# Redrawing the opening third of a written-out order, with one half pair's maximum subtracted on TensorE

## The chip, the cores and the metric

The kernel runs on one core of one Trainium2 chip. The metric is the device time of one execution in microseconds.

## The reference

Two layers follow each other. The first is attention in chunks: q, k and v are of shape (8 batches, 8 heads, 576 positions, 64), and each chunk of 64 positions attends to itself alone. The second takes the result as x of 576 x 512 per batch, multiplies x by a weight matrix, gates it with the sigmoid of a causal convolution of x over five positions, and multiplies by a second weight matrix.

```python
scores = scale * np.matmul(q_c, k_c.transpose(0, 1, 2, 4, 3))
scores = scores - np.max(scores, axis=-1, keepdims=True)
attn = np.exp(scores)
attn = attn / (np.sum(attn, axis=-1, keepdims=True) + 1e-09)
out = np.matmul(attn, v_c)
...
gate = 1.0 / (1.0 + np.exp(-gate_pre))
val = x @ w_val
return (gate * val @ w_out).astype(np.float32)
```

The two weight matrices and the convolution's taps are stored as 64-bit floating-point numbers; everything else has 32 bits.

## The kernel before, in words

The 8 x 576 positions are laid out as nine groups g of 512 positions (0 to 8). A group has two pairs p; a pair holds the heads of 256 of the 512 channels and has two halves b. The whole program is one list of pieces, ORDER, written out in the code: each piece is a short name with its indices, a small function issues its instructions, and every engine executes its own instructions in the order of this list (`run` keeps the program order). No engine overtakes itself, so an instruction that waits holds up everything behind it on its engine. SLOTS gives, in the order of the calls, the buffer that each tile takes; a transfer into a buffer waits until the buffer's last reader is done. All loads and stores are issued by SyncE, in the list's order. In the trace all pieces have one line, L139, that of `run`.

The pieces that matter here, with the engine in brackets:

- `lq`, `lk`, `lv g p [b]` load q, k, v of a pair or of its half (SyncE). `lw n c` loads one of the four row units c of the weights v (first matrix) or o (second), 512 KB each; `lc` loads the taps.
- `w1` to `w9`, `wa`, `wb`, `Q`, `wc` turn the 64-bit words of a unit into a high and a low 32-bit part: `w1` clamps the upper words (VectorE), `w2` scales them (ScalarE), `w3`, `w4`, `w7` work on their bits (VectorE), `w5` scales the lower words (ScalarE), `w8` multiplies them by the exponent (GpSimd, or VectorE as `w8D`), `w6` rounds the high part (ScalarE, or VectorE as `w6D`). The low part is a sum, either on GpSimd or VectorE (`wa`, `wb`) or on TensorE (`Q`, three matmuls that the trace shows as four) and a copy out of PSUM (`wc`).
- `S g p b` computes the scores of a half pair: sixteen small products, 32 records in the trace (TensorE, into PSUM).
- `mx` takes the maximum of each row (VectorE). Then there are two ways: `sb` subtracts it (VectorE), `ex` exponentiates (ScalarE) and `sm` sums and inverts (VectorE); or `ng` scales the maximum by -1/8 (VectorE) and `ea` does exponential, subtraction and sum by ScalarE alone, one exponential and one read-out for each of the 16 (or, of a half, 8) blocks. `ra` and `rr`, or `rc`, then add the small constant and invert.
- `nm` multiplies by the inverse sum (GpSimd; VectorE as `nmD`), `T` transposes (TensorE), `ec` copies the result out of PSUM (ScalarE), `A` multiplies by v (TensorE), `xr`, `xd` and `xc` make x in a high part, a low part and whole (ScalarE, VectorE, ScalarE).
- `V g m c [term]` is one (or, without a term, three) of the matmuls of 128 x 512 of the first weight product: high by high (0), low weight by high x (1), high weight by low x (2). For the first group all terms are listed one by one, in an order of their own. `P` is the same for the second product.
- `k0` and `k` are the taps of the convolution (ScalarE and VectorE), `sg` the sigmoid, `vc`, `gs`, `gr`, `gd` the gating, `oc` and `st` the way out.
- `W n s` keeps TensorE at work with n matmuls of 512 and s of 64 columns on zeros; nothing reads the result.

The opening, which the change redraws, is the first 290 pieces of the list, up to `vc 1 0`; from `V 1 2 3` on the order stays. The first half pairs treated are those of (0, 1), since the weights' units v 3 and v 2 belong to pair 1.

## Time and profile before

| | us |
|---|---|
| median of 3 runs | 280.78 |
| lowest and highest | 280.31, 281.07 |
| span of the profiled execution | 279.6 |
| TensorE, busy in it | 268.9 |
| VectorE, busy in it | 239.5 |
| ScalarE, busy in it | 198.7 |
| GpSimd, busy in it | 59.4 |

The profile is one execution's; its time is given as its span alone, which stands 1.18 us below the median of the runs. In the profile PE is TensorE's matmuls, PEld its weight loads, DVE VectorE, ACT ScalarE, POOL GpSimd and SP SyncE. Tiles are named without their numbers: z and ys are the general buffers, b the PSUM banks, mx and rs the row statistics, e_row the exponentials. A bracket behind an instruction tells how long its engine stood idle before it, and what ended that; "issue" is idle time for which the profile shows no wait. A busy TensorE is not one at its peak, since the ends of matmuls overlap.

### The profile page before, as it was taken

The numbers are of one execution on the slowest core, as the hardware profiler recorded it, in microseconds if no ns is written. First come the engines' busy times: TensorE is split into PE (matmuls) and PEld (weight loads), VectorE is DVE, ScalarE is ACT, GpSimd is POOL, SyncE is SP. The second block draws the span as 40 slices with busy tenths as digits, with TensorE's granted clock in tenths as the row PEclk, the third lists the DMA queues.
The fourth block names the chain that finished last, engine by engine and source line by source line (L and its number), as shares of the span: only waits on it lengthen the run. The fifth ranks groups of instructions, "written<-read, shape, count | busy, mean of one in ns | idle before, by whom it ended". The sixth has DMA issues, their size and how long they took to land.

```text
span 279.6 us, 7851 instructions
## 1 busy us (share of the span) xinstructions
PE 268.9 (96%) x3370; PEld 216.6 (77%) x3370; DVE 239.5 (86%) x303; ACT 198.7 (71%) x368; POOL 59.4 (21%) x58
## 2 busy tenths in 40 slices
...
GB/s 224 395 409 406 406 407 409 290 225 108 281 149 37 192 150 338 189 131 30 2 292 88 2 5 2 0 0 2 0 0 0 4 0 0 16 212 0 241 209 225
DMA packets 14754, 42.46 MB, mean 152 GB/s; under 512 B 1536, under 2 KB 1792, under 8 KB 14720
## 3 DMA queue, kind: packets, MB, share of 16 engines
...
q8 instruction: 26, 0.43, 0.6%
...
## 4 chain that ended last, share of the span: by engine, by line
PE 89%; DMA 8%; issue 1%; SPq 0%; ACT 0%
PE b L139 89%; DMA z<-in_v 4%; DMA z<-in_moe_w_val 2%; DMA z<-in_q 2%; SPq L139 0%; ACT z L139 0%
## 5 line engine op out<-in xcount | busy, mean ns | idle before, releaser
L139 PE MATMUL b<-z,v_hi 128*128 128x512 f32 x288 | 97.3, 403 | 1.3 <-issue 1.1
L139 PE MATMUL b<-o_hi,z 128*128 128x512 f32 (+1 forms) x296 | 94.5, 391 | 0.0
L139 DVE SCALAR_TENSOR_TENSOR ys<-ys,cw 128x511 f32<-128x511 f32 (+7 forms) x104 | 84.5, 863 | 0.1
L139 ACT COPY z<-b 128x1024 f32<-128x1024 f32 (+2 forms) x53 | 50.3, 970 | 38.3 <-PE b L139 35.5
L139 PEld LDWEIGHTS b<-z,v_hi 128*128 128x128 f32 x288 | 53.8, 188 | 14.5 <-issue 1.7
L139 PEld LDWEIGHTS b<-o_hi,z 128*128 128x128 f32 x296 | 55.1, 188 | 12.6
L139 PE MATMUL b<-o_lo,z 128*128 128x512 f32 (+1 forms) x148 | 57.4, 388 | 0.0
L139 PE MATMUL b<-z,v_lo 128*128 128x512 f32 x144 | 55.9, 394 | 0.0
L139 POOL TENSOR_TENSOR z<-e_row,rs 128x1024 f32<-128x1024 f32 (+1 forms) x15 | 27.0, 1804 | 47.2 <-DVE rs L139 17.0
L139 PEld LDWEIGHTS b<-o_lo,z 128*128 128x128 f32 x148 | 27.8, 188 | 5.9
L139 PEld LDWEIGHTS b<-z,v_lo 128*128 128x128 f32 x144 | 27.1, 188 | 5.4
L139 POOL TENSOR_TENSOR z<-ys,z 128x1024 fp32r<-128x1024 f32 x4 | 10.0, 2527 | 96.9 <-ACT z L139 96.9
L139 ACT ACTIVATE ys<-ys 128x1024 f32<-128x1024 f32 x16 | 16.8, 1059 | 11.0 <-DVE ys L139 10.8
L139 ACT ACTIVATE e_row<-b,mx 128x64 f32<-128x64 f32 x80 | 23.7, 345 | 0.4 <-DVE mx L139 0.4
L139 DVE TENSOR_TENSOR z<-b,z 128x1024 fp32r<-128x1024 f32 (+1 forms) x19 | 22.0, 1161 | 2.3 <-ACT z L139 1.3
L139 ACT CAST z<-ys 128x1024 fp32r<-128x1024 f32 x16 | 16.5, 1048 | 9.0 <-DVE ys L139 9.0
L139 DVE TENSOR_REDUCE mx<-b 128x16 f32<-128x1024 f32 (+1 forms) x19 | 21.6, 1144 | 1.3 <-PE b L139 1.1
L139 PEld LDWEIGHTS b<-z,z 64*64 64x64 f32 x960 | 15.7, 135 | 7.8 <-DMA z<-in_k 2.6
L139 PE MATMUL b<-z,z 64*64 64x64 f32 x960 | 17.6, 221 | 3.7 <-DMA z<-in_q 3.0
L139 ACT CAST z<-b 128x1024 fp32r<-128x1024 f32 (+1 forms) x19 | 18.7, 991 | 2.1 <-PE b L139 2.1
L139 ACT ACTIVATE ys<-ys,cw 128x512 f32<-128x512 f32 (+1 forms) x25 | 19.2, 811 | 0.0
L139 ACT ACTIVATION_READ_ACCUMULATOR e_row<-b,mx 128x1 f32 x80 | 19.0, 238 | 0.0
...
## 6 DMA issues: line engine op xcount, KB each, us to landing
...
```

The lines of the kernel that those rows point to most:

```text
L139: return tc.keep_in_program_order(fn(*args, **kwargs))
```

## The change

The list's first 290 pieces are replaced by 285 others, and the buffers in SLOTS are given out anew. The matmuls of the first weight product, the scores, transposes and products with v stay the same in number. Several pieces take another form:

- The first half pair (0, 1, 0) no longer uses `ng`, `ea`, `ra`, `rr`. `mh` splits its maximum into a high and a low part (two small VectorE instructions), `M` subtracts both from the scores in PSUM (four matmuls of 256 columns with minus the identity), `exM` exponentiates the whole half at once, and `sm` sums on VectorE. The second half (0, 1, 1) uses `rc` for `ra` and `rr`, and `nmD` for `nm`.
- For v 1, v 2, v 0 and o 3 a new piece `w58` does `w5` and `w8` in one VectorE instruction. `w1` of v 0 and of all four o units goes to GpSimd (`w1G`). `w2` of v 1 and o 0 goes to VectorE, `w6` of v 3 and v 0 to ScalarE.
- The loads come in another order: q and k of (0, 1, 0) ahead of v 2, the unit v 0 behind v of (0, 1), q and k of (1, 1) and the unit o 3 behind v of (0, 0).
- The three warm matmuls `W 3` move from behind `S 0 1 0` to the start of the list, directly ahead of `W 9 22`.

The functions get an index for half a unit; no piece of the list uses it. The core of the diff, the list up to where it stays and the functions that compute something new:

```diff
-ORDER = """zw,lw v 1,zr 1,zr 0,lc,zi,zs 0,zs 1,lw v 3,lw v 2,w1 v 1,w5 c 0,w1 c 0,w2 v 1,w3 v 1,w5 v 1,w4 v 1,w2 c 0,w3 c 0,w5 v 3,
-w7 v 1,w1 v 3,w6 v 1,w8D v 1,w2 v 3,w4 c 0,w3 v 3,W 9 22,Q v 1,lk 0 1 0,lq 0 1 0,w1 v 2,w4 v 3,w2 v 2,w3 v 2,w5 v 2,w6D v 3,
-S 0 1 0,lk 0 0 0,lk 0 1 1,lq 0 1 1,lq 0 0 0,lk 0 0 1,lq 0 0 1,w4 v 2,wc v 1,mx 0 1 0,w6 v 2,w7 c 0,ng 0 1 0,w7 v 2,ea 0 1 0,ra 0 1 0,
-W 3,S 0 1 1,w8D v 2,S 0 0 0,mx 0 1 1,w8D c 0,w9,ng 0 1 1,w7 v 3,S 0 0 1,lw v 0,lk 1 0,lq 1 0,lv 0 1,lw o 3,ea 0 1 1,ra 0 1 1,
-rr 0 1 0,Q v 2,w8 v 3,mx 0 0,nm 0 1 0,sb 0 0,Q v 3,w5 v 0,w1 v 0,ex 0 0,T 0 1 0,w3 v 0,rr 0 1 1,S 1 0 0,wc v 2,sm 0 0,
-nm 0 1 1,S 1 0 1,ec 0 1 0,w2 v 0,A 0 1 0,lk 1 1,lq 1 1,lv 0 0,lv 1 0,wc v 3,mx 1 0,T 0 1 1,nm 0 0,xr 0 1 0,ec 0 1 1,
-V 0 2 2 0,sb 1 0,V 0 3 2 1,w5 o 3,A 0 1 1,xc 0 1 0,xr 0 1 1,w4 v 0,T 0 0,xc 0 1 1,xd 0 1 0,V 0 2 3 0,w6D v 0,V 0 3 3 0,
-ec 0 0,V 0 2 3 1,w1 o 3,S 1 1 0,w7 v 0,ex 1 0,xd 0 1 1,A 0 0,w8 v 0,k0 0 2,sm 1 0,S 1 1 1,wa v 0,xc 0 0,V 0 0 2 0,V 0 2 2 1,
-V 0 0 3 1,V 0 0 2 1,xr 0 0,mx 1 1,V 0 1 2 0,nm 1 0,V 0 0 3 2,V 0 3 3 1,k0 0 0,V 0 3 2 2,V 0 2 3 2,xd 0 0,V 0 3 1 0,
-V 0 1 2 1,V 0 0 0 0,V 0 3 3 2,V 0 3 0 0,lw o 0,lw o 2,lw o 1,w5 o 0,k0 0 3,ng 1 1,k 0 0 1,T 1 0,k0 0 1,wbD v 0,V 0 0 0 2,
-w2 o 3,V 0 3 2 0,k 0 0 2,V 0 2 1 1,ec 1 0,V 0 2 0 0,V 0 0 1 0,k 0 3 1,V 0 1 0 0,V 0 2 0 1,ea 1 1,V 0 2 0 2,w3 o 3,V 0 2 1 2,
-k 0 1 1,V 0 3 1 1,V 0 0 2 2,V 0 1 1 1,w4 o 3,V 0 3 0 1,V 0 2 2 2,V 0 3 1 2,w1 o 1,A 1 0,k 0 0 3,w7 o 3,w1 o 0,V 0 1 3 2,
-V 0 1 1 2,lk 2 0,k 0 3 2,V 0 0 3 0,V 0 0 0 1,lq 2 0,lq 2 1,V 0 0 1 1,k 0 2 1,V 0 3 0 2,V 0 2 1 0,xr 1 0,rc 1 1,S 2 0 0,
-w1 o 2,S 2 0 1,nm 1 1,vc 0 1,xd 1 0,V 0 1 0 2,V 0 1 3 0,lv 3 1,lv 1 1,lq 8 1,lv 2 1,lk 2 1,lk 4 0,lq 6 1,lq 3 0,lv 2 0,
-lk 3 0,lq 3 1,w6 o 3,V 0 0 1 2,lq 4 0,V 0 1 3 1,mx 2 0,xc 1 0,V 0 1 0 1,V 0 1 1 0,V 0 1 2 2,w8 o 3,T 1 1,lk 3 1,vc 0 0,
-sb 2 0,V 1 2 0,ec 1 1,V 1 0 0,w3 o 1,k 0 2 2,ex 2 0,A 1 1,k 0 1 2,w2 o 2,sm 2 0,S 2 1 0,xr 1 1,S 2 1 1,V 1 1 0,w5 o 2,
-xd 1 1,nm 2 0,w2 o 0,V 1 1 1,w2 o 1,V 1 0 1,mx 2 1,xc 1 1,V 1 3 2,ng 2 1,k 0 3 3,V 1 0 3,ea 2 1,w3 o 2,V 1 0 2,k 0 0 4,
-V 1 1 2,k 0 1 3,T 2 0,w4 o 1,V 1 2 2,w7 o 1,k 0 2 3,V 1 3 3,k 0 1 4,V 1 3 0,k 0 2 4,ec 2 0,V 1 3 1,w4 o 2,V 1 1 3,w3 o 0,
-k 0 3 4,S 3 0 0,sg 0 0,S 3 0 1,rc 2 1,w7 o 2,A 2 0,nm 2 1,mx 3 0,vc 1 0,V 1 2 3,xr 2 0,sb 3 0,V 1 2 1,w8 o 2,sg 0 1,T 2 1,
...
+ORDER = """zw,zr 1,zr 0,W 3,lw v 1,w1 v 1,lc,lw v 3,w1 c 0,w2 c 0,w3 c 0,w3 v 1,w2D v 1,w4 v 1,w7 v 1,w6 v 1,w1 v 3,w2 v 3,W 9 22,w3 v 3,
+w58 v 1,w4 v 3,w7 v 3,lq 0 1 0,lk 0 1 0,S 0 1 0,mx 0 1 0,lw v 2,w1 v 2,zi,zs 1,mh 0 1 0,zs 0,Q v 1,w2 v 2,w4 c 0,lk 0 1 1,
+w3 v 2,lq 0 1 1,S 0 1 1,w4 v 2,w7 v 2,M 0 1 0,wc v 1,exM 0 1 0,w6 v 2,w5 v 3,w8 v 3,lq 0 0 1,mx 0 1 1,w58 v 2,lk 0 0 1,S 0 0 1,
+ng 0 1 1,lk 0 0 0,lq 0 0 0,S 0 0 0,sm 0 1 0,nm 0 1 0,w6 v 3,mx 0 0,Q v 2,Q v 3,ea 0 1 1,T 0 1 0,sb 0 0,lq 1 0,ex 0 0,rc 0 1 1,
+w7 c 0,wc v 2,nmD 0 1 1,lk 1 0,sm 0 0,S 1 0 1,T 0 1 1,ec 0 1 0,S 1 0 0,mx 1 0,lv 0 1,A 0 1 0,ec 0 1 1,A 0 1 1,wc v 3,xr 0 1 0,
+lw v 0,xd 0 1 0,w1G v 0,xr 0 1 1,xd 0 1 1,w2 v 0,sb 1 0,w3 v 0,w4 v 0,xc 0 1 0,nm 0 0,T 0 0,V 0 1 3 2,V 0 1 2 0,xc 0 1 1,
+V 0 1 3 1,w5 c 0,ec 0 0,lv 0 0,V 0 0 3 2,V 0 1 2 1,V 0 3 2 0,A 0 0,ex 1 0,lw o 3,lq 1 1,lk 1 1,S 1 1 0,lk 2 1,S 1 1 1,V 0 2 2 2,
+V 0 2 2 1,w6 v 0,xr 0 0,V 0 0 1 0,V 0 3 0 1,V 0 3 1 0,w1G o 3,xc 0 0,V 0 2 3 1,w8D c 0,V 0 2 0 1,V 0 2 2 0,w7 v 0,w9,V 0 3 2 2,
+w58 v 0,sm 1 0,V 0 3 3 1,xd 0 0,V 0 0 3 1,V 0 1 3 0,V 0 2 0 2,V 0 3 1 1,wa v 0,nm 1 0,T 1 0,mx 1 1,V 0 0 0 0,w2 o 3,V 0 3 0 2,
+wbD v 0,w3 o 3,ng 1 1,V 0 1 2 2,k0 0 1,k 0 1 4,k0 0 3,k 0 3 1,V 0 1 1 2,lw o 2,V 0 2 1 1,V 0 0 1 2,w4 o 3,k 0 1 1,k0 0 0,
+V 0 3 3 2,V 0 1 0 1,V 0 2 1 2,k0 0 2,k 0 0 2,k 0 2 4,V 0 0 2 0,k 0 0 1,w3 o 2,ec 1 0,V 0 3 3 0,V 0 0 2 1,V 0 0 3 0,V 0 1 0 2,
+k 0 1 3,V 0 3 1 2,V 0 0 2 2,ea 1 1,rc 1 1,V 0 0 1 1,V 0 0 0 2,V 0 1 0 0,w1G o 2,V 0 1 1 0,V 0 0 0 1,nm 1 1,V 0 1 1 1,vc 0 0,
+lk 2 0,lq 2 0,S 2 0 0,S 2 0 1,w6 o 3,lv 1 0,A 1 0,mx 2 0,xr 1 0,lw o 0,V 0 2 3 0,V 0 2 0 0,V 0 2 3 2,V 0 3 2 1,lw o 1,w1G o 1,
+w2 o 2,sb 2 0,xd 1 0,V 0 2 1 0,lq 2 1,V 0 3 0 0,vc 0 1,lq 3 1,T 1 1,ec 1 1,w4 o 2,w7 o 3,S 2 1 1,V 1 3 0,k 0 3 3,k 0 0 4,lv 1 1,
+ex 2 0,sm 2 0,A 1 1,S 2 1 0,xc 1 0,V 1 3 1,xr 1 1,V 1 0 0,xd 1 1,w5 o 2,lq 4 0,mx 2 1,lk 3 1,w5 o 0,w2 o 1,ng 2 1,w58 o 3,
+k 0 3 2,xc 1 1,w3 o 1,k 0 1 2,k 0 2 2,V 1 1 1,V 1 3 3,k 0 3 4,lv 2 0,w3 o 0,w4 o 1,V 1 1 2,V 1 0 3,lq 6 1,V 1 2 0,w1G o 0,
+w2D o 0,w7 o 1,V 1 0 1,k 0 0 3,V 1 1 0,ea 2 1,lk 4 0,V 1 0 2,w7 o 2,k 0 2 1,lv 2 1,nm 2 0,T 2 0,V 1 1 3,rc 2 1,lq 3 0,lk 3 0,
+S 3 0 1,lv 3 1,k 0 2 3,S 3 0 0,mx 3 0,ec 2 0,A 2 0,V 1 3 2,nm 2 1,V 1 2 2,vc 1 0,lq 8 1,sg 0 0,V 1 2 3,xr 2 0,sb 3 0,V 1 2 1,
...
     def mh(g, p, b=None):
         m = cols(mxs[g, p, b], b)
-        r = pool.tile([P, 2, 16], F32R, name=f"mr{small['mx'] % 6}")
+        small["mr"] = small.get("mr", 0) + 1
+        r = pool.tile([P, 2, 16], F32R, name=f"mr{small['mr']}")
...
-                            rhs=kk[r, b, c], start=True, stop=True, skip_group_check=True)
+                            rhs=kk[r, b, c], start=each or (first and u == a == 0), stop=True, skip_group_check=True)
...
+    def w1(n, c, b=None, on=V):
+        words(n, c)
+        run(on.tensor_scalar, out=part(wt[n, c], b), in0=part(raw[n, c][1], b).bitcast(F32), scalar1=WIDEST, scalar2=-WIDEST,
             op0=ALU.min, op1=ALU.max)
...
+    def w58(n, c, b=None):
+        run(V.scalar_tensor_tensor, out=rest(n, c, b)[1], in0=part(raw[n, c][0], b), scalar=2.0**-52,
+            in1=part(wt[n, c], b), op0=ALU.mult, op1=ALU.mult)
```

## Rows read from the trace of the kernel before

**Rows 1.** the page, busy us of the engines (share of the span), instructions.
```profile
PE 268.9 (96%) x3370; PEld 216.6 (77%) x3370; DVE 239.5 (86%) x303; ACT 198.7 (71%) x368; POOL 59.4 (21%) x58
```

**Rows 2.** the chain that ended last: start us, us, what.
```profile
13.77 11.88 DMA z<-in_v
...
31.90 52.88 PE b L139 x1014
84.78 0.90 issue
```

**Rows 3.** windows: length, busy us (instructions) by engine, granted clock, DMA share, GB/s.
```profile
5.00:10.00 5.00, 2.35 (x27) 1.03 (x27) 4.23 (x12) 3.91 (x8) 0.00 (x0) 1.00 0.95 344
...
25.00:30.00 5.00, 4.57 (x133) 3.91 (x123) 4.15 (x5) 4.62 (x8) 4.46 (x3) 1.00 1.03 410
```

**Rows 4.** timeline of SyncE's transfers: start us, us, queue, tensor, issues merged.
```profile
13.77 1.67 SPq L139 DMA_DIRECT2D z<-in_v  x2
16.32 3.39 SPq L139 DMA_DIRECT2D z<-in_moe_w_out  x3
20.66 0.33 SPq L139 DMA_DIRECT2D z<-in_k  x1
...
25.66 1.61 SPq L139 DMA_DIRECT2D ys<-in_v  x2
```

**Rows 5.** timeline of TensorE (PE, and PEld its weight loads), 0 to 32 us.
```profile
1.19 4.16 PE L139 MATMUL b<-warm 128*128 128x512 bf16 x31 [1.19 <-DVE warm L139]
...
2.02 0.15 PEld L139 LDWEIGHTS <-warm 128*128 128x128 bf16 x1 [0.28 <-issue]
...
9.82 0.69 PE L139 MATMUL b<-z,z 64*64 64x64 f32 x32 [1.39 <-DMA z<-in_q]
...
14.51 1.12 PE L139 MATMUL b<-z,ident 128*128 128x512 f32 x2
...
17.26 0.63 PE L139 MATMUL b<-ident,z 128*128 128x128 f32 x4
...
22.90 1.06 PE L139 MATMUL b<-ident,z 128*128 128x128 f32 x8 [0.32 <-DVE e_row L139]
...
25.78 1.63 PE L139 MATMUL b<-z,z 64*64 64x64 f32 x96 [0.43 <-DMA z<-in_v]
27.34 0.50 PE L139 MATMUL b<-z,v_hi 128*128 128x512 f32 x1
27.68 0.86 PE L139 MATMUL b<-z,v_lo 128*128 128x512 f32 x3
28.38 0.62 PE L139 MATMUL b<-z,v_hi 128*128 128x512 f32 x2
...
31.90 0.73 PE L139 MATMUL b<-z,v_hi 128*128 128x512 f32 x2 [0.17 <-issue]
```

**Rows 6.** groups of VectorE (DVE) by shape, names and shapes xcount | busy us, mean ns.
```profile
L139 DVE TENSOR_SCALAR z<-z 128x512 uint32<-128x512 uint32 x16 | 6.7, 417 | 0.0
L139 DVE SCALAR_TENSOR_TENSOR z<-z 128x512 uint32<-128x512 uint32 x8 | 5.5, 685 | 0.3 <-ACT z L139 0.3
```

**Rows 7.** timeline, ea 0 1 1, ex 0 0, sm 0 0, nm 0 0.
```profile
14.40 0.29 ACT L139 ACTIVATE e_row<-b,mx 128x64 f32<-128x64 f32 x1
...
17.68 1.04 ACT L139 ACTIVATE e_row<-e_row 128x1024 f32<-128x1024 f32 x1
...
18.82 1.24 DVE L139 TENSOR_REDUCE rs<-e_row 128x16 f32<-128x1040 f32 x1 [0.92 <-ACT e_row L139]
...
20.58 1.90 POOL L139 TENSOR_TENSOR z<-e_row,rs 128x1024 f32<-128x1024 f32 x1 [1.55 <-PE b L139]
```

**Rows 8.** group of GpSimd (POOL) by shape: busy us, mean ns.
```profile
L139 POOL TENSOR_TENSOR z<-z,z 128x512 f32<-128x512 f32 x5 | 7.4, 1479 | 6.0 <-DVE z L139 6.0
```

**Rows 9.** timeline of ScalarE, first of the sixteen ea 1 1 and what follows them.
```profile
32.67 0.32 ACT L139 ACTIVATE e_row<-b,mx 128x64 f32<-128x64 f32 x1
...
37.31 1.12 ACT L139 CAST z<-b 128x1024 fp32r<-128x1024 f32 x1
```

232 lines of the change are left out of this document (129 added, 103 removed), and 12 rows, old and new, of the table z.

## The prediction

> **What bounds the kernel now.** I read the page first. TensorE is busy for 96% of the span [rows 1], which only says that there is little to win unless its work shrinks, so the question is where its 10.7 us of idle time lie. The chain of waits answers it [rows 2]: from 31.90 us TensorE works without a break for 52.88 us, stands 0.90 us at 84.78, and works on to the end. Before 25.65 us the chain runs through transfers (the row of 11.88 us is the last of them). The kernel has thus two parts: an opening of some 26 us in which weights, q and k come in and are prepared, and a TensorE-bound rest whose matmuls the change doesn't touch. A change of the opening is worth what it brings forward the moment from which TensorE has work without a gap; everything behind shifts with it.
>
> In the opening the windows show a second full resource: from 5 to 10 us the DMA engines are at a share of 0.95, from 25 to 30 us still at 1.03 with 410 GB/s [rows 3]. The list of SyncE's transfers shows how they follow each other [rows 4]: counted from the start, issue 28 comes at 25.66 us, just as TensorE stops waiting for the v tile of (0, 0) [rows 5], which is issue 20 (13.77 us). Each issue waits for the landing of the one eight before it, so landings can be read off later issues: the 16th lands at 19.39 (the last of the three issues that the row at 16.32 merges and that ends at 19.71), the 17th at 20.66, the 20th at 25.64.
>
> **The change part by part.**
> *The transfers.* The new order issues as many transfers, in another order, and by the code none of the first twenty waits for a buffer. The 13th to 20th are full 512 KB tiles before and after; so I let the nth land when the nth landed. q and k of the first half pair move ahead of the weights v 2: S 0 1 0, at 9.82 before after a wait of 1.39 us [rows 5], should start near 8.4 (the 3rd and 4th transfers' place). lw v 0 goes from 13th to 16th: 19.4. lv 0 0, on which TensorE waited, goes from 20th to 17th: 20.7, long before its use. The 20th is now lk 1 1, which S 1 1 0 needs.
>
> *The first half pair.* Out go one ng, eight ACT pairs of exponential and read-out, ra and rr; in come two small VectorE copies (mh), four matmuls of 256 columns (M), one exponential of 512 elements (exM), and a VectorE sum (sm). The trace has no M. Four matmuls at half the pitch of a 512-column one (three in 0.70 us before 28.38, [rows 5]) are 0.5 us; were each as slow as one of the eight of Q v 2 and Q v 3 (2.75 us from 14.51 to 17.26), 1.4 us; less than nothing is excluded, as they are added. I take 0.5: they are the shortest of that engine's kind. They stand where TensorE waits for data anyway, so neither end is on the path.
>
> *The weights.* w5 and w8 of four units become one VectorE instruction (w58), w1 of five units goes to POOL, w2 of two to VectorE, w6 of two from VectorE to ACT, nm of the second half from POOL to VectorE. With 0.42 us for a scalar operation and 0.69 for a two-operand one [rows 6]: w58 of v 0 and o 3, which VectorE did not do before, +1.4; nm +0.7; sum of the half pair +0.9; two w2 +0.8; five w1 -2.1; two w6 -0.8; VectorE gets about 1 us more by the end of the redrawn part. ACT gets less: the eight pairs alone were 2.3 us (sixteen take 4.64 us, [rows 9]), and four w5 go as well. VectorE stands idle 0.85 us from 25 to 30 us and 0.77 us from 5 to 10 us [rows 3]; the extra 1 us is covered by such holes, with little to spare, and would be on the path without them.
>
> *The half pairs up to T 0 0.* ea 0 1 1 can't begin before its maximum, for which VectorE is as late as before: 14.4, ending near 16.8, as it did. ex 0 0 came at 17.68, behind w5 v 0 and ra; now it only waits for sb 0 0, about 17.1. Its sum sm 0 0 moves from 18.82 to about 18.2 and is done, with its reciprocal, at 19.7 instead of 20.3 [rows 7]. nm 0 0 runs on POOL, but now behind w1G v 0, which can't start before v 0 has landed at 19.4. A scalar operation on 512 elements is not in POOL's list: 0.42 us below (what VectorE needs for one, [rows 6]), 1.48 us above (POOL with two operands, [rows 8]); I take 0.7, half the upper row, since it reads one operand instead of two. nm 0 0 then runs from 20.1 to 22.0 (1.90 us, [rows 7]), and T 0 0 starts at 22.1 instead of 22.90 [rows 5]. Six V matmuls, the ACT copy ec 0 0 and A 0 0 follow; about 3.1 us later TensorE is at S 1 1 0: 25.2. There it waits for lk 1 1 until 25.64. So w1G may take up to 1.1 us before it costs anything. ACT has a wait for it too: w2 v 0 needs w1G v 0, and both xc of (0, 1), ec 0 0 and with them the first V queue behind it; ACT comes to it only near 21.0, behind ec, wc and both xr, so this wait is hidden as long as w1G takes less than 1.6 us.
>
> *The gain.* I compare the start of the tenth V matmul, since both orders have then done the same work on TensorE. Before: A 0 0 and a block of S still follow the wait at 25.78, and the tenth V starts at 28.38 [rows 5]. After: S 1 1 0 and S 1 1 1 from 25.67, 0.52 us each (96 small records, three blocks, fill 25.78 to 27.34), then the 7th V at 26.71, the tenth 0.81 us on at 27.52. Gain 0.86 us. Behind it, the old order loses 0.17 us at the end of T 1 0 (idle before 31.90); since no data is named as its cause, I count it on neither side. ACT's sixteen ea pairs of (1, 1) take 4.6 us (32.67 to 37.31, [rows 9]); in the new order they start behind ec 1 0 near 32.1 and end near 36.7, A 1 0 needs their bank near 37.1, T 1 1 needs nm 1 1 behind them near 39.1 and is reached near 39.6: close but in time. Further on, A 1 1 waits for ec 1 1 and V 1 3 3 for xd 1 1; by the same counting each may be late by 0.2 to 0.3 us, against as much that the order saves by putting S 2 0 beside A 1 0 (one change of shape on TensorE less). I set these off.
>
> The sum against the profiled execution: 279.6 - 0.86 = 278.7 us of span. The median of the runs is 280.78, 1.2 us above this span, and the same 1.2 us stand around it after: 279.9.
>
> **The clock.** TensorE's first warm matmuls of 512 columns are 0.43 us apart (weight loads of 0.15 us with 0.28 us between, as at 2.02), which is 1.2 GHz; the V matmuls at 0.23 us run at 2.4 GHz, and the window from 5 to 10 us grants 1.00, over the idle 1.39 us before 9.82 too [rows 3, 5]. The three warm matmuls that stood in the middle of the opening (W 3) are now at its start, where the block that ended at 5.35 (1.19 + 4.16) ends 0.7 us later, and the idle stretch up to S 0 1 0 is some 2.3 us. The rows show no fall after 1.39 us; for 2.3 us there is none, so I take no fall and keep the other end for the range. By the Trainium skill (TensorE: Matmul & The Clock Gate, "What's actually happening") the throttled state is the default and activity is what lifts it, so a longer idle stretch speaks against this change; the trace before neither shows nor excludes it. By that rule the third rival below would be the outcome.
>
> **The rivals.**
> *No change (280.6).* The new order leaves POOL, ACT and VectorE almost no slack from T 1 0 to A 1 1, and my counting lets each operation start as soon as it can. For it: the counted waits at A 1 1 and V 1 3 3, the extra 1 us on VectorE, w1G at its upper 1.48 us (T 0 0 0.8 us later, S 1 1 0 0.35 us). Against: ACT loses over 2 us of work, and the window from 25 to 30 us shows idle VectorE. Together 0.7 us: 280.6.
> *The gap at 84.78 goes as well (279.0).* 0.90 us without a named releaser; were it a matter of how instructions fall in TensorE's stream, eight more of them could remove it: 279.9 - 0.9. It could as well stay, which I think likelier.
> *The clock falls (281.8).* Place: the idle stretch before S 0 1 0. It decides if TensorE is still at the lower level when Q v 2 and Q v 3 come, near 14.3. These took 2.75 us (14.51 to 17.26, [rows 5]) and would take 5.5; T 0 1 0, both A 0 1, xr and T 0 0 move by about 2.7 us, of which 0.5 us is hidden by the wait for lk 1 1: S 1 1 0 would come at 27.9 instead of 25.67, and the gain of 0.86 us would turn into a loss of 1.4 us, with everything behind at full clock. If the clock is back after the first of the two Q, half of the 2.75 us falls away and the loss is near zero. I take 1.0: 281.8.
>
> **How the numbers follow.** A measurement of this kernel can tell about 0.3% (0.84 us) from no change. Forecast 279.9: 0.50, spread from 279.3 to 280.4, so slightly more than half of it counts as faster. No change 280.6: 0.24, mostly within 0.3%. Gap gone, 279.0: 0.13, faster. Clock, 281.8: 0.13. Faster: 0.28 of the forecast, 0.02 of the second case, 0.13 of the third: 0.43. Slower: 0.09 of the clock and 0.08 of the second case, if more waits add up than I counted: 0.17. Within 0.3%: the rest, 0.22 + 0.14 + 0.04 = 0.40. The range, 278.9 to 281.4, takes in the third case's value and the forecast's and second case's spread, and of the clock's case the mild half; what it leaves out is that case's other half and a few in a hundred at either end.
>
> **What would show it.** Right: SyncE's 28th issue again near 25.6; T 0 0 near 22.1; TensorE waiting for in_k just before 25.7 and the tenth V near 27.5; granted clock 1.00 and Q v 2 at 1.4 us; from there no TensorE idle above 0.3 us up to the first V of the old order (V 1 2 3, which should come some 0.9 us earlier). Wrong: POOL's w1G over 1.1 us with T 0 0 later than 22.5; matmuls of 512 columns 0.43 us apart near 14 us; waits of TensorE for ACT or VectorE from 30 to 46 us that sum to the gain; VectorE without any idle time through that stretch.

## The result and the profile after

The changed kernel takes **282.69 us** (median of 7 executions, 281.76 to 285.38) against 281.07 (280.31 to 281.70) of the kernel before beside it: a ratio of 1.0076, interval 1.0051 to 1.0100, so 0.8% slower where 0.3% faster was forecast. Three of the 7 had a mean clock of 0.988 to 0.994 and took 283.5 or more; ratios here leave out executions that were over 1.5% above the fastest, so where many were, a median lies above what its ratio says.

The profiled execution (282.69 us, span 280.9, clock 1.0) shows no single culprit. In the changed kernel the line of `run` is L137. TensorE's opening in the timeline, which answers to [rows 5]:

```profile
9.29 0.69 PE L137 MATMUL b<-z,z 64*64 64x64 f32 x32 [3.01 <-DMA z<-in_k]
...
12.54 0.71 PE L137 MATMUL b<-mr,signed 128*128 128x256 f32 x4
...
14.63 0.69 PE L137 MATMUL b<-z,z 64*64 64x64 f32 x32 [0.67 <-DMA z<-in_q]
...
23.02 1.09 PE L137 MATMUL b<-ident,z 128*128 128x128 f32 x8 [1.29 <-POOL z L137]
...
28.27 0.40 PE L137 MATMUL b<-z,v_lo 128*128 128x512 f32 x1
...
30.84 0.27 PE L137 MATMUL b<-ident,z 128*128 128x128 f32 x1
31.39 0.92 PE L137 MATMUL b<-ident,z 128*128 128x128 f32 x7 [0.28 <-issue]
...
44.49 0.93 PE L137 MATMUL b<-z,z 64*64 64x64 f32 x49 [0.17 <-issue]
...
60.40 1.09 PE L137 MATMUL b<-ident,z 128*128 128x128 f32 x8 [1.03 <-POOL z L137]
```

S 0 1 0 (first line) starts at 9.29 instead of the forecast 8.4, T 0 0 at 23.02 instead of 22.1, and the tenth V matmul at 28.27 instead of 27.52. S 0 0 0, the second half of pair (0, 0), starts at 14.63; in the kernel before that pair's second half came at 13.88:

```profile
13.88 0.69 PE L139 MATMUL b<-z,z 64*64 64x64 f32 x32 [0.69 <-DMA z<-in_q]
```

S 1 1 0 waits for no transfer; the forecast had it wait for lk 1 1. What follows is new: two waits "issue", for nothing the profile shows, inside T 1 0 (31.39) and inside A 1 1 (44.49, after 47 of its 64 matmuls), and 1.03 us ahead of T 2 1.

Three points split the loss, because both orders have done the same work at each (the tenth V; V 1 2 3, up to which from the tenth V on both have 53 V pieces, 3 T, 6 S and 3 A; the last matmul):

| | before | after | change | forecast |
|---|---|---|---|---|
| tenth V | 28.38 | 28.27 | -0.11 | -0.86 |
| V 1 2 3, later by | 28.71 | 29.55 | +0.84 | 0 |
| end of the last matmul, later by | 219.58 | 220.12 | +0.54 | 0 |

The chain that ended last answers to [rows 2]:

```profile
56.98 1.07 ACT z L137
...
58.19 2.17 POOL z L137
60.36 0.04 issue
60.40 217.55 PE b L137 x2420
```

From 60.40 us TensorE works to the end without a break: the 0.90 us at 84.78 [rows 2] are gone. So the last row of the table is +1.1 at T 2 1 (2.59 us from V 1 2 3 to it, 1.49 before), -0.9 for that gap, and +0.3 spread thinly.

Three more profiles of the changed kernel were taken in the experiments. In all four the tenth V starts at 27.75 to 28.27 us, so 0.1 to 0.6 of the 0.86 us were gained against the one profile of the kernel before; from there to V 1 2 3 it takes 29.39 to 29.71 us instead of 28.71, and to T 2 1 again 2.59. The first profile, the one shown here, has the latest opening of the four.

SyncE's timeline answers to [rows 4]:

```profile
8.49 1.00 SPq L137 DMA_DIRECT2D z<-in_q  x2
...
11.86 0.33 SPq L137 DMA_DIRECT2D z<-in_moe_w_val  x1
...
20.27 0.33 SPq L137 DMA_DIRECT2D z<-in_q  x1
...
25.37 1.61 SPq L137 DMA_DIRECT2D z<-in_q  x2
```

The first row is the 12th and 13th issue, which wait for the landings of the 4th and 5th (8.48 and 9.15 us). The second is the 16th, the unit v 0 (value-weight chunk 0 from here on); the third, the 24th, waits for its landing: 20.25 instead of 19.39. The 28th issue comes at 25.37, as forecast (25.6). VectorE's and GpSimd's timelines answer to [rows 7, 8]:

```profile
18.99 1.24 DVE L137 TENSOR_REDUCE rs<-e_row 128x16 f32<-128x1040 f32 x1
20.26 0.25 DVE L137 RECIPROCAL rs<-rs 128x16 f32<-128x16 f32 x1
```

```profile
20.43 0.67 POOL L137 TENSOR_SCALAR z<-z 128x512 f32<-128x512 f32 x1 [3.12 <-DMA z<-in_moe_w_val]
21.07 1.90 POOL L137 TENSOR_TENSOR z<-e_row,rs 128x1024 f32<-128x1024 f32 x1
...
49.38 1.08 POOL L137 TENSOR_SCALAR z<-z 128x512 f32<-128x512 f32 x1 [8.00 <-DVE z L137]
50.42 2.09 POOL L137 TENSOR_TENSOR z<-e_row,rs 128x1024 f32<-128x1024 f32 x1
58.18 2.17 POOL L137 TENSOR_TENSOR z<-e_row,rs 128x1024 f32<-128x1024 f32 x1 [5.67 <-ACT z L137]
```

The clamp w1G v 0 took 0.67 us, the 0.7 of the forecast, but nm 0 0 behind it started at 21.07, not 20.1. The sums that nm 0 0 needs were done at 20.51, not 19.7. The last three rows are w1G o 0, nm 2 0 and nm 2 1: the piece on which T 2 1 waits.

### The profile page after: what moved, and what is told of

It is laid out like the page before. It is cut to its first block, busy times and chain, and to the rows that moved or that the text cites. A ratio compares the mean times of both kernels' runs of the same rounds, so it can differ in the third digit from the quotient of the medians.

```text
span 280.9 us, 7856 instructions
## 1 busy us (share of the span) xinstructions
PE 269.7 (96%) x3374; PEld 217.5 (77%) x3374; DVE 244.1 (87%) x313; ACT 194.5 (69%) x348; POOL 60.1 (21%) x60
## 4 chain that ended last, share of the span: by engine, by line
PE 88%; DMA 6%; ACT 2%; POOL 2%; SPq 1%; issue 1%; POOLq 0%
PE b L137 88%; DMA z<-in_moe_w_val 3%; DMA z<-in_q 3%; POOL z L137 2%; SPq L137 1%; ACT z L137 1%; ACT e_row L137 1%; ACT L137 0%; ACT ys L137 0%; POOLq L137 0%
## 5 line engine op out<-in xcount | busy, mean ns | idle before, releaser
L137 PE MATMUL b<-z,v_hi 128*128 128x512 f32 x288 | 97.3, 403 | 0.0
L137 PE MATMUL b<-o_hi,z 128*128 128x512 f32 (+1 forms) x296 | 94.5, 390 | 0.0
L137 ACT COPY z<-b 128x1024 f32<-128x1024 f32 (+2 forms) x62 | 58.4, 961 | 36.5 <-PE b L137 34.4
L137 PEld LDWEIGHTS b<-o_hi,z 128*128 128x128 f32 x296 | 55.2, 188 | 12.7 <-ACT z L137 0.2
L137 PEld LDWEIGHTS b<-z,v_hi 128*128 128x128 f32 x288 | 53.9, 188 | 12.8 <-ACT z L137 0.2
L137 DVE SCALAR_TENSOR_TENSOR z<-z,cw,z 128x511 f32<-128x511 f32 (+3 forms) x80 | 57.7, 763 | 0.0
L137 PE MATMUL b<-o_lo,z 128*128 128x512 f32 (+1 forms) x148 | 57.5, 389 | 0.0
L137 PE MATMUL b<-z,v_lo 128*128 128x512 f32 x144 | 56.4, 395 | 0.0
L137 POOL TENSOR_TENSOR z<-z,z 128x1024 fp32r<-128x1024 f32 (+2 forms) x8 | 16.2, 2027 | 113.7 <-ACT z L137 96.7
L137 POOL TENSOR_TENSOR z<-e_row,rs 128x1024 f32<-128x1024 f32 (+1 forms) x15 | 28.4, 1892 | 32.7 <-DVE rs L137 17.7
L137 PEld LDWEIGHTS b<-o_lo,z 128*128 128x128 f32 x148 | 27.8, 188 | 5.9
L137 ACT ACTIVATE z<-z 128x1024 f32<-128x1024 f32 (+3 forms) x22 | 18.8, 875 | 19.4 <-DVE z L137 19.4
L137 PEld LDWEIGHTS b<-z,v_lo 128*128 128x128 f32 x144 | 27.1, 188 | 5.5
L137 DVE SCALAR_TENSOR_TENSOR ys<-ys,cw 128x1022 f32<-128x1022 f32 (+7 forms) x32 | 31.0, 1002 | 0.0
L137 PE MATMUL b<-z,z 64*64 64x64 f32 x1408 | 25.5, 220 | 4.4 <-DMA z<-in_k 3.0
L137 PEld LDWEIGHTS b<-z,z 64*64 64x64 f32 x1408 | 22.8, 135 | 8.7 <-issue 5.0
L137 DVE TENSOR_TENSOR z<-z,z 128x1024 f32<-128x1024 f32 (+1 forms) x19 | 22.9, 1225 | 2.1 <-PE b L137 1.4
L137 DVE TENSOR_TENSOR z<-b,z 128x1024 fp32r<-128x1024 f32 (+1 forms) x19 | 21.9, 1161 | 3.3 <-ACT z L137 2.7
L137 DVE TENSOR_REDUCE mx<-b 128x16 f32<-128x1024 f32 (+1 forms) x19 | 21.6, 1147 | 1.2 <-PE b L137 1.0
L137 PE MATMUL b<-ident,z 128*128 128x128 f32 x144 | 19.2, 275 | 2.6 <-POOL z L137 2.3
L137 ACT ACTIVATE e_row<-b,mx 128x64 f32<-128x64 f32 x72 | 21.4, 349 | 0.1
L137 PEld LDWEIGHTS b<-ident,z 128*128 128x128 f32 x144 | 16.2, 141 | 5.6 <-POOL z L137 3.5
```

Source lines behind the costliest of these rows:

```text
L137: return tc.keep_in_program_order(fn(*args, **kwargs))
```

## The experiments

All kernels below are the changed kernel with the edit shown; the edits are fragments of the list. Two batches ran on one chip, the later ones on others; each is compared with the kernel before in its own batch, whose median was 280.77 in the first three batches and 281.06 in the fourth. A lowered clock is a mean granted clock of 0.994 or less over an execution, a full one 0.998 or more.

**The changed kernel again.** No edit.

> The changed kernel itself, unchanged, to see what repeats. My theory: the opening repeats in every execution at full clock: v 3 lands near 7.8 us (not 6.3), the first score block starts near 9.3, T 0 0 near 23.0, and TensorE waits some 1.0 us for T 2 1 near 59.4. Runs whose mean clock is 1.000 take 281.7 to 282.7; runs with a clock under 0.997 are 1 us or more slower, and there is at least one of them in five. Rival (the late landing is chance of one profile): v 3 lands before 6.8 here.

283.01 us (281.43 to 284.23, 11 runs), ratio 1.0078 (1.0053 to 1.0104). Five of the 11 had a clock of 0.993 or 0.994 and took 283.66 to 284.23; the six at 0.998 to 1.0 took 281.43 to 283.01. Its profile has the same waits: 0.43 us inside T 1 0, 0.20 inside A 1 1, 1.03 ahead of T 2 1 at 60.05. The opening did not repeat as expected: v 3 landed at 7.14, S 0 1 0 came at 8.82 and T 0 0 at 22.52.

**Chunk 0's clamp on VectorE.**

```diff
-xd 0 1 0,w1G v 0,xr 0 1 1
+xd 0 1 0,w1 v 0,xr 0 1 1
```

> The clamp of unit v 0 goes back from GpSimd to VectorE, at the same place of the list. Theory: nm 0 0 no longer stands behind it and starts when sm 0 0 is done, near 20.55 instead of 21.07, T 0 0 near 22.5 instead of 23.0, S 1 1 0 near 25.9 instead of 26.4: 0.4 to 0.5 us less at the tenth V, and 0.3 to 0.5 us less in all. Rival (VectorE is what decides, it gets 0.4 us more): T 0 0 earlier but no gain, or a loss of up to 0.4 us, since rc 2 1 comes later and T 2 1 waits longer.

282.74 us (281.63 to 286.07), ratio 1.0061 (1.0039 to 1.0083), which the intervals don't tell from 1.0078. T 0 0 started at 22.34, but the V matmuls behind it then waited 0.55 us for ScalarE, whose copies stood behind w2 v 0 and that behind the clamp on VectorE; the tenth V came at 28.40. The wait had moved, not gone.

**The output chunks' clamps on VectorE.**

```diff
-w1G o 3, ... w1G o 2, ... w1G o 1, ... w1G o 0
+w1 o 3, ... w1 o 2, ... w1 o 1, ... w1 o 0
```

> The clamps of the four o units go back from GpSimd to VectorE, at the same places. Theory (VectorE is held up while GpSimd works on a long tile): the tap at 50.7 takes 0.74 us instead of 2.39, the ones at 32.6 and 49.9 lose their 0.4 us each, nm 2 0 starts near 46 instead of 50.4, rc 2 1 comes 1.5 us earlier and the wait of T 2 1 falls from 1.03 to under 0.4 us: 0.6 to 1.0 us less in all. Rival (VectorE simply has too much work): it gets 1.4 us more, rc 2 1 comes later and T 2 1 waits 1.0 us or more: the same time or up to 1 us slower.

281.30 us (280.92 to 283.25), ratio 1.0030 (1.0009 to 1.0050): by the medians 1.7 us below the changed kernel, by those of the executions at full clock 1.0 (281.18 against 282.13). From V 1 2 3 to T 2 1 it takes 1.59 us instead of the 2.59 of the changed kernel beside it. A wait for nothing shown stands at 86.44, 0.68 us long, where the changed kernel has none. This profile happens to be one with a lowered clock; the windows of its opening (length, busy us with counts, granted clock, DMA share, GB/s):

```profile
6.00:8.00 2.00, 0.97 (x24) 0.73 (x22) 0.61 (x3) 0.62 (x1) 0.00 (x0) 1.00 0.90 333
8.00:10.00 2.00, 0.67 (x25) 0.70 (x28) 1.97 (x5) 1.03 (x3) 0.00 (x0) 0.81 1.03 406
10.00:12.00 2.00, 2.00 (x22) 1.11 (x15) 1.75 (x7) 0.42 (x1) 0.00 (x0) 0.50 1.06 399
12.00:14.00 2.00, 2.00 (x38) 1.28 (x37) 1.62 (x4) 0.80 (x2) 0.00 (x0) 0.84 1.05 400
```

Behind the stretch without work ahead of S 0 1 0 (2.36 us here) the clock is at 1.2 GHz (0.50) to about 12.6 us: S 0 1 1 starts at 12.99 instead of 11.91. This execution took 283.25, 1.95 us over the median of its kernel.

**The gap filled, first try.**

```diff
-w2 v 3,W 9 22,w3 v 3
+w2 v 3,W 22 22,w3 v 3
```

> Thirteen warm matmuls of 512 columns more (2.8 us at the higher clock), so that TensorE works until shortly before the first score block. Theory (the idle 3.0 us let the clock fall in a part of the executions): all runs at a clock of 0.999 or more, spread under 1.2 us, median 0.4 to 1.0 us below the changed kernel's, and the opening as it was, T 0 0 near 23.0. Rival (the clock has nothing to do with it): clocks under 0.997 still occur and the median stays within 0.3 us.

286.85 us (285.89 to 288.65), ratio 1.0222 (1.0186 to 1.0258): 4 us slower than the changed kernel, which no theory on record had. S 0 1 0 started in time (9.51), but then, in TensorE's timeline:

```profile
27.54 0.39 PE L137 MATMUL b<-z,v_lo 128*128 128x512 f32 x1
31.25 0.40 PE L137 MATMUL b<-z,v_hi 128*128 128x512 f32 x1 [3.31 <-ACT z L137]
```

The waits written in the program were the same as in the changed kernel, where this V doesn't wait; so ScalarE, named as the releaser, was not likely the cause. Counting helped. The windows from the start to a wait give TensorE's matmuls and weight loads, its records, so far. Changed kernel, to its two waits for nothing:

```profile
0.00:31.20 31.20, 24.36 (x471) 16.82 (x472) 24.68 (x49) 21.52 (x49) 9.46 (x15) 1.00 0.94 360
0.00:44.40 44.40, 37.30 (x724) 27.27 (x725) 37.63 (x70) 33.90 (x90) 12.71 (x18) 1.00 0.97 373
```

The bridged kernel, to its wait:

```profile
0.00:30.00 30.00, 24.96 (x471) 15.92 (x472) 23.65 (x48) 20.40 (x48) 9.18 (x15) 1.00 0.93 357
```

And the kernel before, to the waits at 31.73 and at 84.78:

```profile
0.00:31.80 31.80, 25.04 (x473) 16.69 (x473) 24.37 (x50) 26.71 (x71) 10.46 (x15) 1.00 0.95 364
0.00:85.00 85.00, 77.92 (x1487) 59.77 (x1487) 75.17 (x122) 78.15 (x210) 34.99 (x34) 1.00 0.81 305
```

TensorE stops after record 943 (471 + 472) in both, though the bridge put 26 records ahead of all the work: the place belongs to the instruction stream, not to the data. The other stops are at 1449 = 943 + 2 x 253 and at 946 and 2974, eight times 253.5 apart. In the DMA queues a queue "instruction" moves 26 packets of 16 KB in the whole run; one of them ends 1.35 to 1.6 us ahead of the end of each of these waits (29.92 for 31.39, 29.88 for 31.25, 84.10 for 85.68). So these are **waits for TensorE's own code**, which comes in blocks of some 253 records.

When a packet starts can be read too. In the changed kernel TensorE enters the block ahead of record 943 (its record 690) at 25.69 us; the packet for the next block starts 3.2 us later, takes 1.0, and TensorE goes on 1.5 later, at 31.39. In the profiles of this document the packet starts mostly 3 to 4 us after the entry while transfers run, and mostly about 1 us or less after it behind 55 us, where they run less. In the first bridge, held up by 4 us, both moved together: entry 42.92 and packet 46.31, against 38.82 and 41.95. So a block that TensorE works off in under some 5.7 us (3.2 + 1.0 + 1.5) ends in a wait, and which block holds many small matmuls decides where. The Trainium skill ("Runtime: NRT & Kernel Launch", "Instruction fetch mechanics") has blocks of 16 KiB, 256 instructions, fetched by the sequencer's own queue, and calls the crossing "mostly hidden". Size and queue agree with the trace; hidden it is not here: 0.17 to 3.31 us.

**The gap filled with as many instructions as before.**

```diff
-w2 v 3,W 9 22,w3 v 3
+w2 v 3,W 19 12,w3 v 3
```

> The same 31 matmuls on zeros as in the changed kernel, but 19 of 512 columns and 12 of 64 in place of 9 and 22 (W 19 12), so that TensorE is busy until some 8.5 us and the 3.0 us without work ahead of S 0 1 0 shrink to under 1, with no instruction more or less. Theory (two things were mixed in the earlier bridge: it filled the gap, and it put 13 matmuls with their weight loads, 26 records, ahead of the point where TensorE had run out of code; TensorE waited there 3.3 us, after the same record 943 at which the changed kernel waits 0.28): here the wait after record 943 stays between 0.1 and 0.7 us and ends near 31.0 to 31.5, the tenth V stays within 0.5 us of 28.3, and where part of the runs of the changed kernel had a lower clock from the gap, these have not: median 282.0 to 282.4 and no run above 283.0, where the changed kernel again had 283.0 and runs up to 284.2. Rival one (the bridge itself costs, S 0 1 0 or the clock suffers by it): 284 or more. Rival two (the low clock comes from another place): 282.7 to 283.2 with runs up to 284.

282.35 us (282.06 to 283.25, 6 runs), ratio 1.0059 (1.0038 to 1.0081), every run at a clock of 1.0: as expected but for two runs slightly over 283. So the bridge itself costs nothing, and the 4 us of the first one were the 26 records, which brought TensorE to record 943 at 27.94 us, while the packet came no earlier than in the changed kernel (28.85 and 28.89). In the profiled run (283.25) chunk 0 landed late, at 20.97, and T 0 0 waited 2.15 us.

**The gap filled with fewer instructions.**

```diff
-w2 v 3,W 9 22,w3 v 3
+w2 v 3,W 19,w3 v 3
```

> 19 matmuls of 512 columns on zeros and none of 64 (W 19), so TensorE is as busy in the gap as in the other bridge but has 12 matmuls with 12 weight loads, 24 records, fewer ahead of everything. Theory (TensorE has executed 943 records when it waits for code that lands near 31 us, whatever those records are): the wait lies 24 records later in the work, in the V matmuls behind T 1 0 some 2 to 2.5 us further on, and as the code lands no later than before, the 0.28 us of wait are gone or below 0.1; a wait at record 1449 (0.17 us in the changed kernel) goes as well. Time 0.2 to 0.5 us below the other bridge, 281.6 to 282.1. Rival (the waits are the wait for ScalarE's writes that the profile names for the earlier bridge, not code): the wait stays at the same place in the work, and the time is that of the other bridge within 0.2.

The trace did what the code theory asked: no wait of over 0.1 us at records 943 and 1449. The time did not: 284.25 us (282.05 to 285.45), ratio 1.0129 (1.0104 to 1.0154). The profiled run, 282.05, is the shortest of six. Two of the others had a lowered clock, but three took 283.98 to 285.45 at full clock, and these stay unexplained.

**The short bridge and the output clamps on VectorE.** Both edits.

> The short bridge (W 19) and the clamps of the four output-weight chunks on VectorE instead of GpSimd together. Theory (three losses that add up: GpSimd's clamp of chunk 0 that stands ahead of nm 2 0 and leads to the 1.0 us wait of T 2 1; TensorE's code; the clock after the gap): 280.3 to 281.0, below the changed kernel by 1.7 to 2.5 and level with the kernel before. Rival (the wait of the changed kernel at T 2 1 covers the others, so they don't add): 281.2 to 281.6, as with the clamps alone, 281.3.

Six of 12 runs took 280.34 to 282.19, six 285.0 to 286.92 at a clock of 0.988 to 0.994 (median 283.59, ratio without these 1.0002, 0.9981 to 1.0023). Against the short bridge alone, on the same chip with the same opening, TensorE at T 2 1, clamps on GpSimd:

```profile
59.97 1.09 PE L137 MATMUL b<-ident,z 128*128 128x128 f32 x8 [1.04 <-POOL z L137]
```

and on VectorE:

```profile
58.98 1.09 PE L137 MATMUL b<-ident,z 128*128 128x128 f32 x8
```

The last matmul ends at 276.32 instead of 277.31: the 0.99 us go through to the end. How the clamp makes the wait stands in VectorE's timeline of the changed kernel,

```profile
49.88 0.87 DVE L137 TENSOR_SCALAR z<-z 128x512 uint32<-128x512 uint32 x1
50.67 3.70 DVE L137 SCALAR_TENSOR_TENSOR z<-z,cw,z 128x510 f32<-128x510 f32 x3
...
57.76 0.25 DVE L137 RECIPROCAL rs<-rs 128x16 f32<-128x16 f32 x1
```

against that of this kernel:

```profile
50.09 0.42 DVE L137 TENSOR_SCALAR z<-z 128x512 uint32<-128x512 uint32 x1
50.42 2.06 DVE L137 SCALAR_TENSOR_TENSOR z<-z,cw,z 128x510 f32<-128x510 f32 x3
...
56.34 0.25 DVE L137 RECIPROCAL rs<-rs 128x16 f32<-128x16 f32 x1
```

w1G o 0 waits 8.00 us on GpSimd for VectorE, and nm 2 0, whose sums were done at 45.9, stands behind it. Both then run from 49.4 to 52.5 beside VectorE, where a scalar operation takes 0.87 instead of 0.42 us and three taps 3.70 instead of 2.06. The short bridge alone has the same rows as the changed kernel (0.87 and 3.71 us). With the clamp on VectorE, nm 2 0 runs at 46.73, elsewhere. VectorE reaches the reciprocal for nm 2 1 at 56.34, 0.99 us earlier than in the short bridge alone (57.33), and nm 2 1 starts at 56.72. (For the changed kernel the profile names ScalarE as its releaser, done 0.04 us behind the reciprocal; here that ScalarE instruction ends at 57.99, so nm 2 1 doesn't need it.) The Trainium skill ("GPSIMD Engine Reference", "Specifications") says that the two engines share their way to SBUF and contend where VectorE reads two inputs there or works in what the page calls a 2-port perf mode. The taps here read two inputs; the 0.87 us belong to an operation with one, and its mode no run here shows.

**Without M.** The first half pair as before (ng, ea, rc for mh, M, exM, sm), the rest of the new order.

> The order as in the changed kernel, but the first half pair has its maximum subtracted on VectorE and its exponentials taken in one ScalarE instruction, as in the kernel before (no mh, M, exM, sm for it; ng, ea, rc instead). Theory (M is not what costs; the loss lies in the later part of the new order, and what M gains at the start ends at the wait for code near 31 us): the tenth V comes 0 to 0.8 us later than 28.3, the wait after record 943 shrinks or goes, and the time is within 0.5 us of the changed kernel's 283.0. Rival one (M costs: its wait on VectorE's difference, and its four matmuls): 281.8 or less. Rival two (M gains all the way to the end): 283.6 or more.

284.54 us (282.38 to 288.60, 7 runs), by the letter the number of the second rival. But three of the seven took 286.65 to 288.60 at a clock of 0.987 or 0.988; without them the ratio is 1.0083 (1.0053 to 1.0113) against 1.0078 of the changed kernel. As far as four executions tell, M neither costs nor gains more than some 0.3%, so the subtraction on TensorE isn't where the loss is. Without M the stream is 8 records shorter, and three of seven executions took 285 us or more, instead of one of twenty; none of these was profiled.

**Chunk 0's steps behind nm 0 0.**

```diff
-xd 0 1 0,w1G v 0,xr 0 1 1,xd 0 1 1,w2 v 0,sb 1 0,w3 v 0,w4 v 0,xc 0 1 0,nm 0 0,T 0 0,
+xd 0 1 0,xr 0 1 1,xd 0 1 1,sb 1 0,w3 v 0,xc 0 1 0,nm 0 0,w1G v 0,T 0 0,
-V 0 1 3 2,V 0 1 2 0,xc 0 1 1,
+V 0 1 3 2,V 0 1 2 0,xc 0 1 1,w2D v 0,w4 v 0,
```

> The changed kernel with one weight chunk's steps moved: GpSimd's clamp of value-weight chunk 0 (w1G v 0) behind nm 0 0 instead of ahead of it, its scaling on VectorE (w2D v 0, some 0.45 us) instead of ScalarE and, with w3 v 0 and w4 v 0, behind the subtraction of pair (1,0). Theory (T 0 0 is late because nm 0 0 stands on GpSimd behind the clamp, which waits for a transfer that lands at 20.2 to 21.0, not at the 19.4 of the prediction): nm 0 0 starts at the row sums, near 20.0 to 20.6, T 0 0 at 22.0 to 22.6 (23.03 before), its wait falls from 1.28 us to 0.3 to 0.8, and the tenth V comes at 27.4 to 27.9 (28.27). TensorE then comes earlier to record 943 and waits there longer for code, until 30.9 to 31.4, 0.5 to 1.0 us in place of 0.28, so that of 0.5 us no more than 0.2 is left at A 1 0: time 282.3 to 283.0. Rival one (no wait for code, the gain goes through): 282.0 or less. Rival two (the chunk is then late for its own V matmuls, as the 0.55 us wait was when the clamp went to VectorE): 283.3 or more, with a wait of TensorE for ScalarE or VectorE between 23 and 29.

282.21 us (281.43 to 283.14), ratio 1.0049 (1.0031 to 1.0067). TensorE's timeline (L134 here, since the list takes fewer lines):

```profile
22.20 1.09 PE L134 MATMUL b<-ident,z 128*128 128x128 f32 x8 [0.95 <-POOL z L134]
...
30.35 0.27 PE L134 MATMUL b<-ident,z 128*128 128x128 f32 x1
31.10 0.92 PE L134 MATMUL b<-ident,z 128*128 128x128 f32 x7 [0.48 <-issue]
```

T 0 0 is 0.82 us earlier than in the first profile of the changed kernel; the wait for code ends at 31.10 instead of 31.39, so 0.29 us are left behind it. Against the other three profiles of the changed kernel nothing is left: there T 0 0 came at 22.52 to 22.68, the tenth V at 27.75 to 27.91 (27.78 here) and the end of this wait at 30.90 to 31.11. That the code caps what the opening gains is shown by the first bridge; this pair alone does not show it.

**Three edits together,** wide bridge, output clamps on VectorE and, in the second kernel, chunk 0 behind nm 0 0.

> The wide bridge (W 19 12) and the four output-weight clamps on VectorE. Theory: the two add up, T 2 1 waits under 0.2 us instead of 1.0, and as with the short bridge pair (59.97 to 58.98 at T 2 1, 277.31 to 276.32 at the end) the 1.0 us goes through to the end: 281.1 to 281.5 against the wide bridge's 282.35; a wait of 0.1 to 0.7 us at record 943 or none, by how late T 0 0 is. Rival (the gap of 0.9 us at V 1 2 3's far side that the kernel before has near 84.8 comes back and eats the gain, as in the profile of the clamps alone): 282.0 or more.

281.40 us (280.89 to 283.26), ratio 1.0028 (1.0009 to 1.0048), as expected.

> Wide bridge, output clamps on VectorE, and chunk 0's steps behind nm 0 0, together. Theory: T 0 0 at 22.0 to 22.6 whenever chunk 0 lands, the wait for code at record 943 0.5 to 1.0 us until 30.9 to 31.4; so the gain over the same kernel without the move is small where chunk 0 lands early and 0.5 us or more where it lands late, and the runs lie closer together: 280.8 to 281.2, the highest run at 282.0 or less. Rival one (nothing caps it): 280.3 or less. Rival two (no gain): the other's time within 0.2.

281.31 us, all 12 runs from 280.72 to 281.41, ratio 1.0006 (0.9992 to 1.0020): the steadiest form, level with the kernel before. The median is that of the form without the move; what went are the executions above 281.6, four of 12 there.

**The same with the short bridge, and one in between (W 19 6).**

> The same three edits with the short bridge (W 19), so with 24 records fewer ahead of record 943. Theory (the code that lands near 31 us is what stops the early gain, and 24 records are 2.3 us of V matmuls): no wait at record 943 or one under 0.2 us, the 0.5 us of T 0 0 go through to the end: 279.8 to 280.3 in its undisturbed runs, 0.5 to 0.9 below the wide form and 0.5 below the kernel before. Rival one (code does not cap): equal to the wide form within 0.2. Rival two (with fewer small matmuls at the start the lower clock comes in half the runs, as it did in 6 of 12 before): the median is 282 or more whatever the undisturbed runs give.

280.92 us (280.50 to 287.37), ratio 0.9993 (0.9975 to 1.0012); 4 of 12 runs at 286 or more. In the profile (280.71) the tenth V comes at 27.54, which is the forecast's 27.52, and still V 1 2 3 at 57.08, where it was before (57.09). The eight shorter executions, 280.50 to 281.30, are 0.5 to 1.0 us above what was expected.

> The three edits with a bridge between the two forms: 19 matmuls of 512 columns and 6 of 64 (W 19 6), 12 records fewer ahead of record 943 than the wide form, 12 more than the short one. Theory (a wait for code of 0.2 us goes with 12 records, some 1.2 us of V matmuls, and the long runs belong to the short form's place of the block ends): 280.6 to 281.1 with no run over 282. Rival one (12 records decide nothing): 281.3, as in the wide form. Rival two (it is the bridge's end that brings the long runs): a third or more of the runs at 285 or more.

283.25 us (280.42 to 288.50), ratio 0.9995 (0.9971 to 1.0018); 7 of 14 runs at 285 or more: the wide form's steadiness is already lost with 12 records fewer.

**A long execution in profile.** The short bridge with the clamps, three more times, unchanged.

> One look at the kernel with the short bridge and the output clamps on VectorE, unchanged, of whose 12 runs 6 took 280.3 to 282.2 us and 6 took 285 to 287 at a mean clock of 0.988 to 0.994. Theory (in the long ones TensorE runs out of code for 3 us or more, as in the first bridge, and the clock is halved behind that wait): if this profile is a long one it has a wait of 3 us or more for nothing the profile shows, behind the end of a 16 KB code block, with a stretch of granted clock 0.5 right behind it. Rival (the clock falls in the 0.5 us without work ahead of S 0 1 0, as in the profile of the clamps alone, 8 to 14 us): the low clock begins before 14 us and no such wait is seen. If it is a short one: 280.3 to 281.5, and nothing is told apart.

> The same kernel once more, as a second chance to see a long run: the expectations are those of the first look.

> The same kernel a third time: the expectations are those of the first look.

286.56, 285.62 and 286.46 us: all three are long ones. In the chain that ended last, the first shows

```profile
41.51 2.66 PE b L137 x94
44.17 3.23 issue
47.41 92.70 PE b L137 x1395
```

and in its windows

```profile
0.00:46.00 46.00, 40.11 (x724) 28.21 (x725) 39.28 (x74) 34.31 (x90) 10.73 (x15) 1.00 0.96 374
```

```profile
44.00:47.40 3.40, 0.17 (x10) 0.04 (x2) 2.19 (x4) 0.34 (x1) 0.94 (x1) 0.91 1.03 407
47.40:49.00 1.60, 1.59 (x38) 1.47 (x38) 0.00 (x0) 1.01 (x2) 0.96 (x1) 0.50 1.03 410
49.00:51.00 2.00, 2.00 (x6) 1.52 (x6) 1.96 (x2) 2.00 (x5) 0.00 (x0) 0.50 1.03 412
```

It is the wait after record 1449 (724 + 725), 3.23 us long, and behind it TensorE at 1.2 GHz to beyond 51 us. The other two profiles have 3.23 and 3.51 us at the same record, the profile of the form in between 3.35. The rival, a fall ahead of S 0 1 0, is excluded for these. The code packet of that block starts at 44.97 here; in the undisturbed profile of the same kernel it starts at 41.78 and TensorE doesn't wait. TensorE entered the block ahead at 38.20 here and at 38.51 there: in the four long executions the packet starts 6.8 to 7.0 us after that, otherwise 3.1 to 3.4. What delays it stays open: in both it shares the engines with transfers at a DMA share of 1.03.

**The changed kernel, profiled twice more.**

> One look at the changed kernel as it is, of whose 18 runs so far 8 had a mean clock of 0.988 to 0.994 and took 283.5 to 285.4 us, the others 281.4 to 283.0. Theory (its long runs are those of the short bridge, smaller: the code behind record 1449 lands late): a profile of 283.5 or more has a wait of 1 us or more behind record 1449, near 44 to 47, instead of 0.17 to 0.2, and the granted clock falls behind it. Rival (the gap of 3 us ahead of S 0 1 0): the clock is low between 8 and 14 us, as in the profile of the clamps alone, and the wait at record 1449 is under 0.5. A profile under 283.2 tells nothing apart.

> The changed kernel a second time, with the expectations of the first look at it.

281.93 and 282.34 us at a clock of 1.0 and 0.998: neither is a long one, so nothing is told apart.

## Why the prediction was wrong

It put 279.9, and 282.69 came, outside its range. Two steps failed. The gain of 0.86 us at the tenth V was sized too large (0.1 to 0.6 us came), and "everything behind shifts with it" did not hold: nothing of it arrived at V 1 2 3, and at T 2 1 another 1.1 us went, since the clamps' move to GpSimd was followed to its end for the first clamp alone.

Of the 2.8 us, 2.2 are span (280.9 instead of 278.7) and 0.6 the margin around it: I added the 1.2 us between the median and the one span of before, and 1.8 stand around every execution of the changed kernel, 1.9 to 2.0 around the later ones of the kernel before. So before's profiled execution was probably a long one itself, by some 0.7 us, and the two profiles, 1.3 us apart, show less than the 1.6 to 2.2 us between the medians. At full clock the medians are 282.13 (12 executions) and 280.63 (61): 1.5 us.

*The transfers.* At S 0 1 0 the count failed, not the rule "I let the nth land when the nth landed": its q and k are the 4th and 5th transfers of the new list, not the 3rd and 4th. The 12th and 13th issues, which wait for these, come at 8.49 and 9.17, in the kernel before at 8.38 and 9.03. The rule itself failed further on: the 12th transfer, on which S 0 0 0 waits, came 0.75 us later than the 12th before, and chunk 0 was there at 20.25, not 19.39. In the four profiles of the changed kernel chunk 0 landed at 19.76 to 20.25, in those of its variants at 19.31 (without M) to 20.97 (the wide bridge), and with the clamp ahead of nm 0 0 each of these moved T 0 0.

*The half pairs up to T 0 0.* Two paths were late. The sums of pair (0, 0) were to be done at 19.7 and were at 20.51, behind the late S 0 0 0, so that nm 0 0 could not have started before 20.5 even without the clamp; the clamp, waiting for chunk 0, added the other 0.5 us. The price of w1G (0.7) was right, its cover too small: "up to 1.1 us" counted from the forecast landing. The wait for lk 1 1 that was to hide it didn't occur. M, 0.5 expected, took 0.71, beside waits, as said.

*The gain.* The sum "everything behind shifts with it" failed. With all opening delays taken out (tenth V at 27.54) nothing of 0.84 us was left at V 1 2 3. In the changed kernel itself a large part of the +0.84 on that stretch are the code waits inside T 1 0 and at record 1449: 0.45 us of idle time together against 0.17 before, and 0.81 against 0.41 from start to start (0.55 us between two transposes that are else 0.11 apart, 0.39 between two matmuls of A that are else 0.01 to 0.04 apart), since the modelled end of a matmul hides part of a wait. The rest is spread: matmuls of 512 columns start 234 ns apart in the median instead of 231 (over 70 of them, 0.1 to 0.2 us). In the short form with all three edits 0.83 us are lost there too: 0.3 us ahead of T 1 0, a wait of 0.32 us at 41.4, 0.1 at record 1449, and the spread; their causes were not tried.

*The clamps.* I priced five w1 on GpSimd as 2.1 us taken off VectorE and looked at the first alone. The step that failed is the one that asks what is queued behind a waiting instruction: w1G o 0 waits for VectorE with nm 2 0 behind it. That is 1.0 us, shown by the pair of short bridges.

*The clock.* The third rival (281.8, chance 0.13) was too small in both numbers. Of 20 executions of the changed kernel, 8 had a lowered clock and took 283.5 to 285.4, some 1.7 us more than the others. All 30 timed runs of the three wide-bridge kernels, with as many records and the gap filled, were at 0.998 or above. That points to the gap ahead of S 0 1 0, as the windows of the clamp kernel show for one execution. Its length alone does not decide: the changed kernel kept the full clock over 3.01 us in its first profile and the clamp kernel lost it over 2.36. Nor is it the longer gap that brings the low clock: the kernel before, with 1.39 us, had one in 34 of 95 executions, but there these took 281.2 us against 280.6, only 0.5 more. What changed is what a fall costs; why was not tried.

*The gap at 84.78.* The second rival was right in its mechanism, "how instructions fall in TensorE's stream": record 2974 is the end of a block. That the gap went, giving back 0.9 us of the other losses, is not owed to eight records more. In the changed kernel that block ends at record 2969, which TensorE reaches 1.1 us later (85.88, 1.38 us behind the end of its packet), just when the code is there. With the output clamps on VectorE the wait came back at the same record, 0.68 us long (86.44).

*The first rival* named A 1 1 and V 1 3 3 as the likely place of new waits, for data. TensorE waited at neither for data; the 0.17 us inside A 1 1 are for code.
